# Fourier filter and two-layer MLP on one core: the second transform stage and the stage behind the filter as four 64x64 tiles of TensorE

## The chip, the cores and the metric

The kernel runs on one core of one Trainium2 chip. The metric is the device time in microseconds of one execution. The engines are TensorE (PE, with its weight loads as PEld), VectorE (DVE), ScalarE (ACT), GpSimd (POOL) and SyncE (SP, which here only issues DMAs). Each runs its own instructions in program order and waits for the others by semaphores.

## The reference

For each of 8 batches of 3008 tokens by 256 channels: a real FFT along the tokens, a product with a complex filter, and the inverse FFT. The 24064 tokens then go through a two-layer MLP with a leaky ReLU between.

```python
X = np.fft.rfft(x, axis=1)
F = (filt_r + 1j * filt_i)[None, :, :]
y = np.fft.irfft(X * F, n=x.shape[1], axis=1)
x = y.reshape(B * S, D)             # 24064 x 256
h = x @ w_in                        # 256 x 2048
g = np.maximum(0.01 * h, h)
out = g @ w_out                     # 2048 x 256
```

## The kernel before

**The transform.** 3008 is written as N1 x N2 = 94 x 32, so each FFT is two stages of matmuls, and so is each inverse. Only 48 values of k1 are kept, in two sets of 24. A batch from 1 on goes through these groups; each writes one bank of PSUM, which ACT or DVE empties:

- `s1_group` (L254): the first stage, 16 groups of one matmul over 94 rows (L259), copied by ACT (L262) and stored to DRAM (`dz1`, L264).
- `t1_load` (L268): the result comes back turned, so that a column of TensorE's input holds the 32 values of n2 for four quarters (real and imaginary parts of the two sets of k1): `z1`, four places.
- `s2_group` (L302): the second stage, 12 groups of two matmuls of 128x128 by 256 columns (L308). Half of each 128x128 weight is zero, since the two sets of k1 do not mix. The filter is then applied: DVE multiplies the bank by `fb_sb` (L317) and `fa_sb` (L320), two DMAs swap the two 64-partition halves of the first product (L318, L319), and POOL adds (L323).
- `sa_group` (L326): the stage behind the filter, 12 groups of one matmul of 512 columns (L330), copied by ACT (L332) and stored to DRAM (`dz2`, L334).
- `t2_load` (L275) and `sb_group` (L343): back from DRAM, turned again, and the last stage, 16 groups of four matmuls (L351), copied by ACT into `yt` (L341).

**The MLP.** The tokens are taken in 47 chunks of 512. `moe1` (L514) makes two blocks of 128 hidden channels in a wide PSUM bank pair, with the leaky ReLU on ACT behind every second block (L519). From chunk 3 on the second product is made in seven products of half size (`products`, L589) with sums on DVE (L555, and one add for each product).

**The order.** It is written out by hand. Every step is put at a time of a plan, in units of which a chunk has SL = 8, and the program is emitted in the order of these times: `moe1` steps stand 0.5 units apart, the products evenly between them. `plan` (L694) gives the transform groups of a batch their due times (a start and a step for each kind, in PLANS); the loop at L741 takes them in that order, at least GAP = 0.6 units apart, and not before their loads have landed by plan. `soon` puts the follow-up steps (swaps, adds, stores) some units behind.

**The banks.** `bank` (L156) gives out PSUM. "ph" means two wide banks in turn, shared by `moe1`. "pf" means single banks: the one that the plan marks free first is taken, and its mark is moved on by a hold. After the first chunk two single banks are left for all the transform groups (L499, L500); two more serve the products.

```python
i = min(range(len(single)), key=lambda i: frees[i])
t, frees[i] = single[i], max(frees[i], clock["now"]) + hold
```

Batch 0 has an order of its own (`FIRST`), with other tiles; there some matmuls are 128*64, two column halves side by side (L401 and L442).

Of the kernel before, what the change touches and what calls it, by code (L numbers as in the profile page):

```python
# [11 lines left out]
P = 128  # L12
# [8 lines left out]
NC = 24  # L21
Q = 32
R1 = 96
FP = 3


def _build_np_constants(N):
    n1, n2 = np.arange(N1), np.arange(N2)
    h = N2 // 2

    k2 = np.concatenate([np.arange(h), np.arange(N2 - 1, h - 1, -1)])

    sg = np.where(k2 < h, 1.0, -1.0)[None, :]
    th = 2 * np.pi * np.outer(n2, k2) / N2
    co, si = np.cos(th), np.sin(th)

    fwd1 = np.zeros((P, P))
    fwd2 = np.zeros((P, NC, P))
    inv1 = np.zeros((P, N2, N1))
    inv2 = np.zeros((P, P))  # L40

    for s, (qr, qi) in enumerate(((0, 2), (1, 3))):
        k1 = NC * s + np.arange(NC)

        cr, ci = (slice(64 * i + s, 64 * i + 64, 2) for i in range(2))
        r, i = (slice(Q * q, Q * q + Q) for q in (qr, qi))
        ang = 2 * np.pi * np.outer(n1, k1) / N1
        fwd1[:N1, qr * Q : qr * Q + NC] = np.cos(ang)
        fwd1[:N1, qi * Q : qi * Q + NC] = -np.sin(ang)
        for c in range(NC):  # L50
            t = th + 2 * np.pi * n2[:, None] * k1[c] / N
            fwd2[r, c, cr], fwd2[i, c, cr] = np.cos(t), np.sin(t)
            fwd2[r, c, ci], fwd2[i, c, ci] = -np.sin(t) * sg, np.cos(t) * sg

        w = np.where((k1 == 0) | (k1 == N1 // 2), 1.0, 2.0)[:, None] / N1
# [5 lines left out]
        inv2[cr, i], inv2[ci, i] = si.T, (co * sg).T  # L61
    inv2 /= N2
# [9 lines left out]
    return tuple(np.ascontiguousarray(t).astype(np.float16) for t in (fwd2, inv1, small, fwd2t, inv1t))  # L72


@with_exitstack
def kernel(
# [41 lines left out]
    )  # L118

    f2_np, i1_np, small_np, f2t_np, i1t_np = _build_np_constants(N)  # L120
# [4 lines left out]
    i1t_d = nc.inline_tensor(i1t_np, name="inv1t_const")  # L125

    cpool = ctx.enter_context(tc.tile_pool(name="const", bufs=1))
    f2_sb = cpool.tile([P, NC, P], FP16, name="f2_sb")
# [3 lines left out]
    fb_sb = cpool.tile([P, NC, D], FP16, name="fb_sb")  # L132
    w_in_sb = cpool.tile([P, NDT, DFF], FP16, name="w_in_sb")
    w_out_sb = cpool.tile([P, NCT, D], FP16, name="w_out_sb")
    wt_sb = cpool.tile([P, 4, NCH, P], FP16, name="wt_sb")
    x_sb = cpool.tile([P, N2, D], FP16, name="x_sb")
    big = [cpool.tile([P, Q * D], FP16, name=f"big{i}") for i in range(3)]
# [31 lines left out]
    def at(time, f):  # L169
        clock["n"] += 1  # L170
        heapq.heappush(work, (time, clock["n"], f))
# [96 lines left out]
    def t1_load(b, c):  # L268
        def go():
            need(*[("st1", b, h) for h in range(8)], *[("s2", b, 2 * c - 7)] * (c > 3))  # L270
            nc.sync.dma_start(z1[c % 4], turned(dz1[b % 2], N2, c))
            issued.add(("z1", b, c))
        return go

# [51 lines left out]
    def sa_group(b, g):  # L326
        def go():
            ps = bank("pf", 2, D)
            need(("y", b, g), *[("st2", b, g // 2 - 4)] * (g > 7))
            nc.tensor.matmul(ps, inv2, ys.pop((b, g))[:], start=True, stop=True)  # L330
# [5 lines left out]
        return go  # L336

    def quad_copy(h, dt, ps, copy):

# [164 lines left out]
    def moe1(ci, ct):  # L504
        g, j = divmod(ct, 2)
        if ct == 0:
            gts[ci] = gtp.tile([P, NCT, CH], FP16, tag="gt", name=f"gt_c{ci}")
        if j == 0:
            phs[0] = bank("ph", 2, CH)
        ph, t = phs[0], ci * CH  # L510
        while t < (ci + 1) * CH:
            e = min((ci + 1) * CH, (t // N + 1) * N)
            for dt in range(NDT):
                nc.tensor.matmul(ph[:, j, ds(t - ci * CH, e - t)], w_in_sb[:, dt, ts(ct, P)],  # L514
                                 yt[:, dt, ds(t % N, e - t)],
                                 start=(dt == 0), stop=(dt == NDT - 1))
            t = e
        if j == 1:
            nc.scalar.activation(gts[ci][:, ds(2 * g, 2), :], ph, AF.Lrelu)  # L519
# [174 lines left out]
    def plan(b, s1, s1_step, s2, s2_step, lag, sb, sb_step, xl, x_step):  # L694
        for g in range(16):
            groups.append((s1 + s1_step * g, 1, b, g, s1_group(b, g, dve if b == 1 and g % 4 < 3 else act)))
            if g % 2 and b + 1 < B:
                at(s1 + xl + x_step * g, lambda g=g: (need(("s1", b, g)), noted(
                    ("x", b + 1, g // 2), lambda: x_load(b + 1, 2 * g - 2, 4))))
        for g in range(12):  # L700
            groups.append((s2 + s2_step * g, 2, b, g, s2_group(b, g)))
            groups.append((s2 + lag + s2_step * g, 3, b, g, sa_group(b, g)))
        first_use[1, b], first_use[3, b] = s2, sb
        for g in range(16):
            due = SL * (QT * (8 * b + g // 2) // CH)
            groups.append((min(sb + sb_step * g, due - DUE[0] + DUE[1] * (g % 2)), 4, b, g, sb_group(b, g, act)))

    for i, (o, i0, i1) in enumerate(wt_sums):
        at(10 + 0.5 * i, lambda o=o, i0=i0, i1=i1: nc.vector.tensor_tensor(o, i0, i1, AL.subtract))

# [17 lines left out]
    def load_time(stage, b, c):  # L728
# [7 lines left out]
            at(t, (t1_load if stage == 1 else t2_load)(b, c))  # L736
        return loads[stage, b, c]

    queue = [(time, n, *v) for n, (time, *v) in enumerate(groups)]
    heapq.heapify(queue)  # L740
    while queue:  # L741
        time, n, stage, b, g, f = heapq.heappop(queue)
        t = max(time, last + GAP)
        if stage == 3:
            behind = when[2, b, g] + y_delay(b, g) + 0.02 if (2, b, g) in when else None
        else:
            behind = load_time(stage - 1, b, g // 2) if stage != 1 else 0
            if stage != 1 and behind is not None:
                behind += READ
        if behind is None or behind + 0.02 > t:  # L750
            heapq.heappush(queue, (t + GAP if behind is None else behind + 0.03, n, stage, b, g, f))
# [5 lines left out]
        assert stage < 4 or t < SL * (QT * (8 * b + g // 2) // CH), (b, g, t)  # L757

    for ci in range(NCHUNK + 1):
# [45 lines left out]
```

## Time and profile before

| | |
|---|---|
| time, median of 3 runs | 746.75 us (746.65 to 747.35) |
| the profiled execution's own time | 747.4 us |
| its span, first to last instruction | 745.2 us |
| PE busy | 738.0 us, 99% of the span |
| PE weight loads | 528.9 us, 71% |
| DVE, ACT, POOL busy | 504.6, 559.1, 166.2 us |
| granted clock of TensorE | 0.999 |
| DMA | 113.64 MB, mean 152 GB/s |

Busy times are unions of an engine's instructions. Matmuls are pipelined, so a row's mean duration (379 ns for 512 columns) is longer than the time from one start to the next. In the timeline a row gives the start, the length from the first start to the last end, and how many instructions were merged. In the windows each engine has its busy time and its number of instructions, then follow the clock, the mean share of the DMA engines that is busy (packets can overlap, so over 1 is possible) and GB/s. Lines are those of the kernel before.

### The profile page before, as it was taken

To read this page: it belongs to the slowest core of one execution; us is meant where nothing else is said; L and a number is where in the kernel's file an instruction comes from. 1 tells how busy PE (TensorE), PEld (TensorE's weight loads), DVE (VectorE), ACT (ScalarE), POOL (GpSimd) and SP (SyncE) were. 2 spreads that over 40 slices of the span, in tenths; PEclk is the share of its full clock that TensorE was granted. 3 is DMA by queue.
4 is the path that set the end of the run, shared out by engine and by line. 5 is a ranking of instruction groups with operands and counts; after the bars stand their busy time and mean duration, and the time that the engine had idled before them with its cause. 6 is when DMAs were issued, how large, how long until landed. Compare 5 with 4: busy or idle time off the path is not lost.

```text
span 745.2 us, 19416 instructions
## 1 busy us (share of the span) xinstructions
PE 738.0 (99%) x8017; PEld 528.9 (71%) x8017; DVE 504.6 (68%) x686; ACT 559.1 (75%) x755; POOL 166.2 (22%) x171
## 2 busy tenths in 40 slices
PE   9999999999999999999999999999999999999997
PEld 3556667677687777877778777777777777777776
DVE  5987637766776766766777667766677676465566
ACT  4776787888878787877777787787777777777762
POOL 6503412332232212121232222121212210000000
PEclk9999999999999999999999999999999999999999
DMA  9997797888876666655675656543554333111012
GB/s 207 229 224 197 191 224 216 209 195 208 216 181 147 159 186 176 169 138 163 193 178 150 159 155 175 156 139 109 144 160 119 106 103 103 60 55 55 29 46 70
DMA packets 119848, 113.64 MB, mean 152 GB/s; under 512 B 16384, under 2 KB 93056, under 8 KB 119568
## 3 DMA queue, kind: packets, MB, share of 16 engines
q1 hardware_dynamic: 104425, 94.73, 42.9%
q0 software_dynamic: 15056, 17.49, 15.8%
q8 instruction: 62, 1.02, 0.6%
q14 instruction: 26, 0.21, 0.1%
q10 hardware_dynamic: 279, 0.19, 0.1%
HBM read 57.51 MB, written 50.33 MB: 145 GB/s over the span
## 4 chain that ended last, share of the span: by engine, by line
PE 96%; DMA 1%; DVE 1%; ACT 1%; issue 0%; ACTq 0%; DVEq 0%
PE ph L514 43%; PE pf L589 18%; PE po_ps L589 18%; PE pf L259 3%; PE pf L351 3%; PE pf L308 2%; PE pf L330 2%; PE po_ps L373 1%; PE pf L681 1%; PE po_ps L681 1%; DMA dz<-big 1%; DMA big<-dz 0%; ACT yt L341 0%; PE pf L442 0%; PE ph L401 0%
## 5 line engine op out<-in xcount | busy, mean ns | idle before, releaser
L519 ACT ACTIVATE gt_c<-ph 128x1024 f16<-128x1024 f32 x376 | 385.3, 1025 | 133.5 <-PE ph L514 122.8
L514 PE MATMUL ph<-yt,w_in_sb 128*128 128x512 f16 (+7 forms) x1728 | 447.3, 351 | 0.2 <-ACT yt L341 0.2
L589 PEld LDWEIGHTS <-gt_c 128*128 128x128 f16 x2800 | 202.2, 98 | 91.1
L323 POOL TENSOR_TENSOR y_b_g<-p_b_g,p_b_g 128x512 f16<-128x512 f32 x84 | 116.4, 1388 | 414.9 <-DMA p_b_g<-p_b_g 249.9
L589 PEld LDWEIGHTS <-big 128*128 128x128 f16 x2128 | 151.2, 98 | 61.4
L514 PEld LDWEIGHTS <-w_in_sb 128*128 128x128 f16 x1728 | 137.5, 98 | 19.7 <-DVE yt L341 0.4
L317 DVE TENSOR_TENSOR p_b_g<-pf,fb_sb 128x512 f32<-128x512 f32 x78 | 53.7, 688 | 31.0 <-PE pf L308 13.8
L589 PE MATMUL po_ps<-wt_sb,gt_c 128*128 128x128 f16 x704 | 70.0, 219 | 0.0
L589 PE MATMUL pf<-wt_sb,gt_c 128*128 128x128 f16 x688 | 68.4, 219 | 0.0
L589 PE MATMUL pf<-w_out_sb,gt_c 128*128 128x128 f16 x720 | 67.9, 219 | 0.0
L589 PE MATMUL pf<-wt_sb,big 128*128 128x128 f16 x704 | 67.2, 219 | 0.0
L262 ACT CAST big<-pf 128x512 f16<-128x512 f32 x98 | 57.1, 588 | 11.9 <-PE pf L259 10.5
L589 PE MATMUL po_ps<-w_out_sb,gt_c 128*128 128x128 f16 x688 | 66.0, 219 | 0.0
L589 PE MATMUL po_ps<-wt_sb,big 128*128 128x128 f16 x688 | 65.3, 219 | 0.0
L341 ACT CAST yt<-pf 128x376 f16<-128x376 f32 x120 | 56.4, 473 | 10.9 <-PE pf L351 8.0
L555 DVE TENSOR_TENSOR big<-gt_c 128x2048 f16<-128x2048 f16 (+1 forms) x46 | 58.7, 1276 | 0.1
L555 DVE TENSOR_TENSOR gt_c<-gt_c 128x2048 f16<-128x2048 f16 x43 | 57.4, 1335 | 1.0
L320 DVE TENSOR_TENSOR p_b_g<-pf,fa_sb 128x512 f32<-128x512 f32 x84 | 57.2, 681 | 0.2
L555 DVE TENSOR_TENSOR big<-gt_c,big 128x2048 f16<-128x2048 f16 (+1 forms) x45 | 55.3, 1230 | 0.0
L555 DVE TENSOR_TENSOR big<-big,gt_c 128x2048 f16<-128x2048 f16 (+1 forms) x45 | 55.2, 1227 | 0.1
L332 ACT CAST big<-pf 128x512 f16<-128x512 f32 x84 | 49.0, 584 | 4.9 <-PE pf L330 3.0
L259 PE MATMUL pf<-x_sb,small_sb 94*128 94x512 f16 x109 | 41.6, 381 | 0.0
(97 smaller groups left out, 625.9 us busy)
## 6 DMA issues: line engine op xcount, KB each, us to landing
dz<-big SPq DMA_DIRECT2D x98, 256.0 KB
p_b_g<-p_b_g SPq DMA_DIRECT2D x156, 128.0 KB
out_dram<-ost_c_h SPq DMA_DIRECT2D x118, 128.0 KB
big<-dz SPq DMA_DIRECT2D x42, 256.0 KB
big<-dz SPq DMA_DIRECT2D x56, 192.0 KB
x_sb<-in_x_dram POOLq DMA_DIRECT2D x40, 192.0 KB, 4.4
x_sb<-in_x_dram POOLq DMA_DIRECT2D x2, 768.0 KB, 9.1
w_in_sb<-in_moe_w_in_dram POOLq DMA_DIRECT2D x1, 1024.0 KB, 13.2
```

Source lines behind the costliest of these rows:

```text
L259: nc.tensor.matmul(ps, fwd1[:N1], x_sb[:N1, ds(2 * g, 2), :], start=True, stop=True)
L262: copy(st[:, ds(2 * (g % 2), 2), :], ps)
L317: nc.vector.tensor_tensor(p2[:], ps, fb, AL.mult)
L320: nc.vector.tensor_tensor(p1[:], ps, fa, AL.mult)
L323: ("y", b, g), lambda: nc.gpsimd.tensor_tensor(y1[:], p1[:], p3[:], AL.add)))
L332: nc.scalar.copy(st2[h % 4][:, ds(2 * (g % 2), 2), :], ps)
L341: copy(yv, ps.rearrange("p c a -> p a c"))
L351: nc.tensor.matmul(ps[:, j, :], z2[h % 4][:K4, j, ts(dt, P)], i1_sb[:K4, 4 * h + j, :], start=True, stop=True)
L514: nc.tensor.matmul(ph[:, j, ds(t - ci * CH, e - t)], w_in_sb[:, dt, ts(ct, P)], yt[:, dt, ds(t % N, e - t)], start=(dt == 0), stop=(dt == ...
L519: nc.scalar.activation(gts[ci][:, ds(2 * g, 2), :], ph, AF.Lrelu)
L555: nc.vector.tensor_tensor(*(v[:, ds(c0, n)] for v in (o, i0, i1)), op)
L589: nc.tensor.matmul(of[t], a()[:, c, ts(t, P)], w[:, c, :], start=(c == 0), stop=(c == NCH - 1))
```

## The change

From batch 2 on (`QUARTERS = 2`) `s2_group` and `sa_group` are gone. In their place 37 visits stand at fixed times of the plan (`VISITS`). A visit makes the second stage of four pairs of k1 (`forward`) and, of the visit before, the stage behind the filter (`backward`), with weights of 64x64: TensorE's rows are split by the set of k1, its columns by the parity of the pair, so four tiles stand side by side. The quarters are arranged anew, so that a set's real and imaginary parts are neighbours, and the turned load follows.

- `forward` takes both single banks, with holds of 1.0 and 2.0, and issues 8 matmuls of 256 columns.
- `filtered`, once for each bank, the second 1.05 units later: two multiplies on DVE, four swaps of 32 partitions instead of two of 64, one add on POOL.
- `backward` takes a wide bank pair and issues 4 matmuls of 512 columns; one ACT copy of 128x1024 empties it.
- Other groups keep away from a visit, from 0.9 units before to 1.0 after (`AROUND`); the three `moe1` steps behind a visit are moved on by 0.35, 0.1 and 0.1 (`PAIRS`).
- `refills`, from 29.4 on: the filter tables are loaded again in the new arrangement (eight casting DMAs on POOL's queue, two DMAs between partitions on SP's, four negations on DVE), and two weight tables (SP).

```diff
-    for s, (qr, qi) in enumerate(((0, 2), (1, 3))):
+    for s, (qr, qi) in enumerate(((0, 1), (2, 3))):
...
+    QUARTERS = 2
+    VISITS = (44.75, 49.75, 55.75, 60.75, 65.75, 71.75) + tuple(8 * c + 4.75 for c in range(9, 40))
+    AROUND = (0.9, 1.0)
+    HOLDS = (1.0, 2.0)
+    PAIRS = (0.35, 0.1, 0.1)
+    SECOND = 1.05
+    ADDED = 1.4
+    STORED = 1.2
+    REFILL = 29.4
...
+            if b >= QUARTERS:
+                src = bass.AP(tensor=src.tensor, offset=src.offset, ap=[[Q * D, 4], [P * D, N2], [1, 4 * D]])
...
+    def refill(dst, src, par, k, first, sgn):
+        nc.gpsimd.dma_start(
+            dst[H * par + 16 * k : H * par + 16 * k + 16],
+            bass.AP(tensor=src.tensor, offset=src.offset + (first + sgn * par) * D,
+                    ap=[[N1 * D, N2 // 2], [sgn * NC * D, 2], [sgn * 2 * D, NC // 2], [1, D]]))
+    def refills():
+        t = REFILL
+        for dst, src in ((fb_sb, filt_i), (fa_sb, filt_r)):
+            for par in range(2):
+                for k, (first, sgn) in enumerate(((0, 1), (N1, -1))):
+                    at(t, lambda v=(dst, src, par, k, first, sgn): refill(*v))
+                    t += 0.7
+        for par in range(2):
+            lo = H * par
+            at(t + 2.5, lambda lo=lo: nc.sync.dma_start(fa_sb[lo + Q : lo + H], fa_sb[lo : lo + Q]))
+            for k in range(2):
+                v = ts(k, NC // 2)
+                at(t + 2 + 1.1 * (2 * par + k), lambda lo=lo, v=v: nc.vector.tensor_scalar(
+                    fb_sb[lo + Q : lo + H, v], fb_sb[lo : lo + Q, v], -1.0, None, AL.mult))
+        at(REFILL, lambda: nc.sync.dma_start(i2q_sb[:], i2q_d.ap()))
+        at(REFILL, lambda: noted(("f2q",), lambda: nc.sync.dma_start(f2q, f2q_d.ap())))
+    def forward(b, v):
+        need(("z1", b, v), ("f2q",))
...
+        ps = [bank("pf", 2, D, hold) for hold in HOLDS]
+        for j in range(2):
+            for s in range(2):
+                for par in range(2):
+                    c = 2 * j + par
+                    nc.tensor.matmul(ps[s][ts(par, H), j, :], f2q[ts(s, H), 4 * v + c, :],
+                                     z1[v % 4][ts(s, H), c, :], start=True, stop=True)
+        for s in range(2):
+            if s:
+                soon(SECOND, lambda: filtered(b, v, 1, ps[1]))
+            else:
+                filtered(b, v, 0, ps[0])
+    def filtered(b, v, s, ps):
+        p1, p2, p3 = (scrp.tile([P, 2, D], FP32, tag=f"p{i}", name=f"p{i}_b{b}_v{v}{s}") for i in (1, 2, 3))
+        nc.vector.tensor_tensor(p2[:], ps, fb2[:, s, ds(2 * v, 2), :], AL.mult)
+        for lo in range(0, P, Q):
+            to = lo ^ Q
+            soon(AFTER[1], lambda lo=lo, to=to: nc.sync.dma_start(p3[to : to + Q], p2[lo : lo + Q]))
+        nc.vector.tensor_tensor(p1[:], ps, fa2[:, s, ds(2 * v, 2), :], AL.mult)
+        ys[b, v, s] = y = ypp.tile([P, 2, D], FP16, tag="y", name=f"y_b{b}_v{v}{s}")
+        soon(ADDED, lambda: noted(("yq", b, v, s), lambda: nc.gpsimd.tensor_tensor(y[:], p1[:], p3[:], AL.add)))
+    def backward(b, v):
+        need(("yq", b, v, 0), ("yq", b, v, 1), *[("st2", b, v - 4)] * (v > 3))
+        ps = bank("ph", 2, CH)
+        y = [ys.pop((b, v, s)) for s in range(2)]
+        for par in range(2):
+            for s in range(2):
+                nc.tensor.matmul(ps[ts(s, H), par, :], i2q_sb[ts(par, H), :],
+                                 y[s][ts(par, H)].rearrange("p j d -> p (j d)"), start=True, stop=True)
+        nc.scalar.copy(st2[v % 4].rearrange("p (j w) d -> p w j d", w=2), ps.rearrange("p w (j d) -> p w j d", j=2))
+        soon(STORED, lambda: noted(("st2", b, v), lambda: nc.sync.dma_start(
+            dz2[b % 2][ds(4 * v, 4)].rearrange("k p d -> p k d"), st2[v % 4])))
+    def visit(i):
+        b, v = QUARTERS + i // 6, i % 6
+        if b < B:
+            forward(b, v)
+        if i:
+            backward(b - (v == 0), (v - 1) % 6)
...
-        t = max(time, last + GAP)
+        t = max([time, last + GAP] + [v + AROUND[1] for v in visits if -AROUND[0] < max(time, last + GAP) - v < AROUND[1]])
...
+    later = {}
+    for t in visits[1:]:
+        for n, v in enumerate(PAIRS):
+            later[2 * int(t) + 2 + n] = v
...
-                at(SL * ci + 0.5 * ct, lambda ci=ci, ct=ct: moe1(ci, ct))
+                at(SL * ci + 0.5 * ct + later.get(NCT * ci + ct, 0), lambda ci=ci, ct=ct: moe1(ci, ct))
```

More of the change, by code (lines that the diff above doesn't have):

```diff
@@ L23 @@
 R1 = 96
+H = 64
 FP = 3
@@ L40, in _build_np_constants @@
     inv2 = np.zeros((P, P))
-    for s, (qr, qi) in enumerate(((0, 2), (1, 3))):
+    fwd2q = np.zeros((P, NC, H))
+    inv2q = np.zeros((P, H))
+    for s, (qr, qi) in enumerate(((0, 1), (2, 3))):
         k1 = NC * s + np.arange(NC)
@@ L53, in _build_np_constants @@
             fwd2[r, c, ci], fwd2[i, c, ci] = -np.sin(t) * sg, np.cos(t) * sg
+            fwd2q[r, c, :Q], fwd2q[i, c, :Q] = np.cos(t), np.sin(t)
+            fwd2q[r, c, Q:], fwd2q[i, c, Q:] = -np.sin(t) * sg, np.cos(t) * sg
         w = np.where((k1 == 0) | (k1 == N1 // 2), 1.0, 2.0)[:, None] / N1
@@ L61, in _build_np_constants @@
         inv2[cr, i], inv2[ci, i] = si.T, (co * sg).T
+        inv2q[r, :Q], inv2q[i, :Q] = co.T / N2, -(si * sg).T / N2
+        inv2q[r, Q:], inv2q[i, Q:] = si.T / N2, (co * sg).T / N2
     inv2 /= N2
@@ L71, in _build_np_constants @@
     fwd2 = fwd2.reshape(P, FP, NC // FP, P).transpose(1, 0, 2, 3)
-    return tuple(np.ascontiguousarray(t).astype(np.float16) for t in (fwd2, inv1, small, fwd2t, inv1t))
+    return tuple(np.ascontiguousarray(t).astype(np.float16) for t in (fwd2, inv1, small, fwd2t, inv1t, fwd2q, inv2q))
 @with_exitstack
@@ L118 @@
     )
-    f2_np, i1_np, small_np, f2t_np, i1t_np = _build_np_constants(N)
+    f2_np, i1_np, small_np, f2t_np, i1t_np, f2q_np, i2q_np = _build_np_constants(N)
     f2_d = nc.inline_tensor(f2_np, name="fwd2_const")
@@ L125 @@
     i1t_d = nc.inline_tensor(i1t_np, name="inv1t_const")
+    f2q_d = nc.inline_tensor(f2q_np, name="fwd2q_const")
+    i2q_d = nc.inline_tensor(i2q_np, name="inv2q_const")
     cpool = ctx.enter_context(tc.tile_pool(name="const", bufs=1))
@@ L134 @@
     w_out_sb = cpool.tile([P, NCT, D], FP16, name="w_out_sb")
+    i2q_sb = cpool.tile([P, H], FP16, name="i2q_sb")
     wt_sb = cpool.tile([P, 4, NCH, P], FP16, name="wt_sb")
@@ L270, in go @@
             need(*[("st1", b, h) for h in range(8)], *[("s2", b, 2 * c - 7)] * (c > 3))
-            nc.sync.dma_start(z1[c % 4], turned(dz1[b % 2], N2, c))
+            src = turned(dz1[b % 2], N2, c)
+            if b >= QUARTERS:
+                src = bass.AP(tensor=src.tensor, offset=src.offset, ap=[[Q * D, 4], [P * D, N2], [1, 4 * D]])
+            nc.sync.dma_start(z1[c % 4], src)
             issued.add(("z1", b, c))
@@ L336, in sa_group @@
         return go
+    f2q = f2_sb[:].rearrange("p (a c) m -> p a c m", a=2)[:, 0].rearrange("p c (e m) -> p (c e) m", e=2)
+    fa2, fb2 = (f[:].rearrange("p (s j) d -> p s j d", s=2) for f in (fa_sb, fb_sb))
+    def refill(dst, src, par, k, first, sgn):
[3 more added lines that the diff above has]
+                    ap=[[N1 * D, N2 // 2], [sgn * NC * D, 2], [sgn * 2 * D, NC // 2], [1, D]]))
@@ new lines, in forward @@
+    def forward(b, v):
+        need(("z1", b, v), ("f2q",))
+        for g in (2 * v, 2 * v + 1):
+            issued.add(("s2", b, g))
+        ps = [bank("pf", 2, D, hold) for hold in HOLDS]
[10 more added lines that the diff above has]
+                filtered(b, v, 0, ps[0])
@@ L699, in plan @@
                     ("x", b + 1, g // 2), lambda: x_load(b + 1, 2 * g - 2, 4))))
[L700 to L703, printed above, removed]
+        if b < QUARTERS:
+            for g in range(12):
+                groups.append((s2 + s2_step * g, 2, b, g, s2_group(b, g)))
+                groups.append((s2 + lag + s2_step * g, 3, b, g, sa_group(b, g)))
+        first_use[1, b], first_use[3, b] = s2 if b < QUARTERS else VISITS[6 * (b - QUARTERS)], sb
         for g in range(16):
@@ L706, in plan @@
             groups.append((min(sb + sb_step * g, due - DUE[0] + DUE[1] * (g % 2)), 4, b, g, sb_group(b, g, act)))
+    refills()
     for i, (o, i0, i1) in enumerate(wt_sums):
@@ L737, in load_time @@
         return loads[stage, b, c]
+    visits = VISITS[: 6 * (B - QUARTERS) + 1]
+    for i, t in enumerate(visits):
+        at(t, lambda i=i: visit(i))
+        for g in range(2):
+            when[2, QUARTERS + i // 6, 2 * (i % 6) + g] = t
+    for b in range(QUARTERS, B):
+        when[3, b, 11] = visits[6 * (b - QUARTERS) + 6] + STORED - AFTER[4]
     queue = [(time, n, *v) for n, (time, *v) in enumerate(groups)]
@@ L757 @@
         assert stage < 4 or t < SL * (QT * (8 * b + g // 2) // CH), (b, g, t)
+    for i, t in enumerate(visits):
+        b, v = QUARTERS + i // 6, i % 6
+        if b < B:
+            ready = load_time(1, b, v)
+            assert ready is not None and ready + READ < t, (b, v, ready, t)
+            place[1, v % 4] = t + 0.1
+    later = {}
+    for t in visits[1:]:
+        for n, v in enumerate(PAIRS):
+            later[2 * int(t) + 2 + n] = v
     for ci in range(NCHUNK + 1):
```

## The prediction

> **What bounds the kernel now.** I read the page first, then the groups by form of the tensor engine (PE), its timeline around the only column-tiled matmuls, the timelines of PE and the scalar engine (ACT) in one steady stretch, the chain of waits around 100 us, and the windows there.
>
> ```profile
> span 745.2 us, 19416 instructions
> PE 738.0 (99%) x8017; PEld 528.9 (71%) x8017; DVE 504.6 (68%) x686; ACT 559.1 (75%) x755; POOL 166.2 (22%) x171
> ...
> PE 96%; DMA 1%; DVE 1%; ACT 1%; issue 0%; ACTq 0%; DVEq 0%
> ```
>
> PE is both the busy engine and 96% of the chain that ended last. From 150 us to 700 us the windows show it busy for 50.00 us in every 50, at a granted clock of 1.00. So a PE microsecond saved is one off the span, and a PE wait added is one on it; no other engine hides either.
>
> ```profile
> L308 PE MATMUL pf<-big,f_sb 128*128 128x256 f16 x168 | 32.1, 273 | 0.2 <-ACT big L262 0.2
> L330 PE MATMUL pf<-y_b_g,small_sb 128*128 128x512 f16 x84 | 31.8, 379 | 0.0
> ```
>
> L308 is the second transform stage, L330 the one behind the filter. Mean durations overlap their neighbours; what one costs is its busy time added to a full engine. In the timeline below two L514 matmuls start at 270.94 and the next work at 271.37, so 512 columns cost 0.216 us. Seven L589 matmuls take 269.51 to 269.90: 0.056 us for 128 columns. 256 columns are then 0.109.
>
> **Part 1, the tiles: what PE gains.** Two old groups are four L308 and two L330 matmuls: 4 x 0.109 + 2 x 0.216 = 0.868 us. One visit is eight matmuls of 256 columns, in two rounds of four tiles, and four of 512 in one round: 2 x 0.109 + 0.216 = 0.434 us if four 64x64 tiles stream together. The trace has no 64-row matmul. The nearest rows are column tiles (128*64):
>
> ```profile
> 21.43 0.60 PE L425 MATMUL pf<-prod,small_sb 128*128 128x512 f16 x2
> 21.96 0.65 PE L401 MATMUL ph<-big,f_sb 128*64 128x128 f16 x16
> 22.55 0.60 PE L425 MATMUL pf<-prod,small_sb 128*128 128x512 f16 x2
> 23.09 0.64 PE L401 MATMUL ph<-big,f_sb 128*64 128x128 f16 x16
> 23.66 0.61 PE L425 MATMUL pf<-prod,small_sb 128*128 128x512 f16 x2
> ```
>
> From 22.55 to 23.66 is 1.11 us, for 2 x 0.216 and eight column pairs. If a pair costs the 0.056 of one matmul, that is 0.88, and 0.23 is left for leaving and re-entering the full array. Were pairs serial, 16 x 0.056 alone would exceed the 0.57 between 23.09 and 23.66. So column halves do run together, and each visit pays 0.23 for its two switches (forward and backward share one stay). Bounds for a round of four: 0.109 if row halves overlap as column halves do, 0.218 if they do not. I take the first, because the two row halves read different partitions and write different banks. Saving: 0.868 - 0.434 - 0.23 = 0.20 us, times 36, less 0.23 for the 37th visit: **-7.1 us**.
>
> The Trainium skill (TensorE: Matmul & The Clock Gate, Part 3) gives 3.07 times for four row tiles, not 4. By that, as an estimate, a visit would stream 0.57 and the saving would be some 2 us. No run here shows it.
>
> **Part 2, the banks: what PE waits for.** This is where I expect the loss. Only two single banks are left for all transform groups after the list is cut at SL - 0.4. A visit takes both, with holds of 1.0 and 2.0 plan units (a unit is 1/8 chunk, about 1.9 us: chunks start 15.2 us apart around 300 us). AROUND keeps every other group out from 0.9 before to 1.0 after. I laid the due times of s1_group and sb_group (the plan's starts and steps) against VISITS by the diff's own rule. 36 of 37 visits get a group A at exactly +1.0, and 27 a second, B, at +1.6. Example: visit 132.75; sb of batch 3, g=1, is due at 132.68 and goes to 133.75; s1 of batch 5, g=8, is due at 133.75 and goes 0.6 behind it, to 134.35. A takes the first bank (free by plan at +1.0) and marks it to +1.75. B chooses the smaller mark, 1.75 against 2.0, so the bank A has just filled, 0.6 units later. Before, two neighbours alternated, and no bank came back under 1.2 units.
>
> On PE, between the starts of A and B lie A itself (0.18 for four L351, 0.22 for one L259), eight products (0.45) and one moe1 step (0.43): **1.06 or 1.10 us**. How long A holds the bank is seen here, first PE, then ACT:
>
> ```profile
> 270.94 0.59 PE L514 MATMUL ph<-yt,w_in_sb 128*128 128x512 f16 x2
> 271.37 0.39 PE L589 MATMUL po_ps<-w_out_sb,gt_c 128*128 128x128 f16 x4
> 271.59 0.38 PE L259 MATMUL pf<-x_sb,small_sb 94*128 94x512 f16 x1
> ```
> ```profile
> 271.57 1.02 ACT L519 ACTIVATE gt_c<-ph 128x1024 f16<-128x1024 f32 x1
> 272.49 0.58 ACT L262 CAST big<-pf 128x512 f16<-128x512 f32 x1
> ```
>
> The second half of a moe1 pair ends just before the group, so its 1.02 us activation stands ahead of the group's copy on ACT, and the bank is free at 273.07, 1.48 us after the matmul started. In a visit PAIRS puts that half at +0.85 and A at +1.0, so two products lie between instead of four, and the copy ends 0.11 later: 1.59 for s1. For sb the copy is 473 ns instead of 588 (L341 and L262 on the page): 1.48. With 0.05 for the semaphore (a copy of the chain ends at 64.92, its matmul starts at 64.97), B waits 0.54 us behind an s1 and 0.47 behind an sb. By the plan A is s1 8 times and sb 19 times: 8 x 0.54 + 19 x 0.47 = **+13.3 us**. Bounds: nothing, if A and B fall further apart than I count; 27 x 0.65 = 18 if ACT is later still.
>
> The Trainium skill (TensorEngine Tiling, PSUM Bottleneck) warns that tiling speeds up TensorE and not the emptying of PSUM. The rows above agree: the copies keep their length while PE comes sooner.
>
> Other waits of a visit I set at nothing, with their cover. The wide bank for the backward half was read one pair earlier; the bank of the pair before is due back 1.53 us after that pair's last matmul starts (0.216 + 4 products + the visit + 8 products) and takes 0.416 + 1.02 to empty: tight, and 0.1 x 37 = 4 us if it slips. DVE keeps two multiplies per half. ACT gives up two copies of 584 ns for one of 1025.
>
> **Part 3, the refills.** At 29.4 (91 us) eight cast DMAs enter POOL's queue, 192 KB each, and four transfers SP's. They fall on a stretch with no slack:
>
> ```profile
> 100.69 5.51 DMA dz<-big
> 106.21 2.98 DMA big<-dz
> ```
> ```profile
> 95.00:100.00 5.00, 5.00 (x41) 3.14 (x40) 3.11 (x4) 4.61 (x8) 1.98 (x4) 1.00 1.00 190
> 100.00:105.00 5.00, 5.00 (x48) 3.21 (x47) 2.44 (x3) 5.00 (x9) 0.00 (x0) 1.00 1.08 275
> 105.00:110.00 5.00, 4.84 (x53) 3.20 (x52) 1.26 (x3) 4.23 (x7) 0.00 (x0) 1.00 0.64 184
> ```
>
> DMA share is 1.0 already, and PE waits 0.16 us for the last of batch 1's z2 loads at 109.2. 1.6 MB of refills at the 190 to 275 GB/s seen is 6 to 8 us of transfer within some 14 us. On POOL's queue the refills also stand ahead of the last y add of batch 1 (94.2, read at 99.3) and of an x load issued at 95.5. Bounds 0 and +8, since other transfers may absorb all of it; I take **+2**, nearer nothing, because the load falls to 0.64 right behind.
>
> **Part 4, the swaps and loads.** SP issues eight swaps of 32 partitions per visit instead of four of 64. Its timeline gives about 0.5 us for each, so +2 us of issue per visit on a queue whose issues fill some 27 of 50 us (31 between 150 and 200). Behind them queue z loads and output stores. Batch 2's visits stand 5 or 6 units apart, some 10 us, and the second y is ready about 9 us after its visit (filter +2, multiply 1.4, four issues 2, landing 2, add 1.4). From batch 3 on the gap is 15 us. The last backward of a batch moves to the next batch's first visit, so z2 loads come just in time at five batch ends. Bounds 0 and +5; I take **+1.5**.
>
> **Sum.** The profiled execution took 747.4 (span 745.2 and 2.2 around it), 0.65 above the median 746.75. 747.4 - 7.1 + 13.3 + 2 + 1.5 = 757.1; less 0.65, **756.5 us**.
>
> **Rivals.** *The gain comes through*: B falls later than I count or ACT is earlier, and the refills hide. For it: PE's saving is plain arithmetic, and DVE, ACT and SP all have spare time on average. Against: the bank rule and the ACT order. Time: 746.75 - 7.1 = 739.7, up to 745 with the small waits. It decides if fewer than 7.1 / 0.5 = 14 visits have a waiting B. *Row halves do not overlap*: streaming stays 0.868 and the switches are added, 37 x 0.23 = +8.5; alone 755, with the banks and the rest 772. For it: no row shows 64-row tiles; against it, column halves do overlap. *A draw*: about half of the bank waits, within 0.2% of 746.75; that much is about what a measurement of this kernel can tell from no change.
>
> **Chances.** Bank waits outweigh the saving 0.60; row halves serial 0.09 (slower too); gain 0.26; draw 0.05. The range 740 to 767 takes in the gain almost whole, the draw, and the forecast with its bounds on banks and refills, and leaves out most of the serial case. For the likeliest case alone it is 749 to 767.
>
> **What would show it.** Right: matmuls of L259 and L351 behind visits with idle time ended by ACT, some 27 gaps of 0.45 to 0.65 us, PE's busy share below 50.00 from 150 us on, and visits about 0.66 us long. Refill wrong: the sb matmul near 109 us not later. Saving wrong: rounds of four taking 0.22. The forecast falls if PE stays gapless between 150 and 640 us.

## The result, and the profile after

The changed kernel took **835.39 us** (median of 6 runs, 831.93 to 837.25) against 747.35 for the kernel before: ratio 1.1178 [1.1153, 1.1202]. It is 88 us slower; the forecast was 756.5 in a range of 740 to 767. The profiled execution has a span of 832.8 us, 87.6 more than before.

First the page of the kernel after: the span, the busy times, and the chain that ended last.

```profile
span 832.8 us, 20090 instructions
PE 757.5 (91%) x8233; PEld 530.3 (64%) x8233; DVE 521.0 (63%) x690; ACT 555.0 (67%) x719; POOL 174.3 (21%) x179
...
PE 74%; DMA 17%; issue 3%; ACT 2%; SPq 2%; POOL 1%; DVE 1%; POOLq 0%; ACTq 0%; DVEq 0%
```

PE was 96% of the chain and is 74%; DMA went from 1% to 17%, the DMA queue of SP from nothing to 2%. Next the groups by form: behind the second bar the idle time of PE ahead of them, and what ended it.

```profile
L278 PE MATMUL pf<-x_sb,small_sb 94*128 94x512 f16 x109 | 42.6, 391 | 8.5 <-DMA x_sb<-in_x_dram 5.3 <-ACT yt L435 3.2
L445 PE MATMUL pf<-i_sb,big 96*128 96x94 f16 x448 | 39.4, 211 | 26.7 <-DMA big<-dz 22.3 <-ACT big L281 2.6 <-ACT yt L435 1.8
L419 PE MATMUL ph<-y_b_v,i2q_sb 64*64 64x512 f16 x144 | 16.8, 390 | 21.0 <-POOL y_b_v L411 21.0
L395 PE MATMUL pf<-big,f_sb 64*64 64x256 f16 x288 | 15.1, 284 | 11.5 <-DMA big<-dz 11.5
```

L395 is `forward`, L419 `backward`, L445 `sb_group`, L278 `s1_group`. "big<-dz" is a load of `z1` or `z2`; L411 is POOL's add, which needs the swapped halves. So some 55 us of PE's idle time (22.3 + 21.0 + 11.5) hang on turned loads and swaps, and only 3.2 + 2.6 + 1.8 = 7.6 on ACT, where the forecast put the loss. The windows show where PE's clock went too (the columns are those of the windows before; the clock stands third from last):

```profile
200.00:250.00 50.00, 36.26 (x380) 24.48 (x378) 24.10 (x34) 26.41 (x34) 9.04 (x9) 0.83 0.56 146
250.00:300.00 50.00, 49.02 (x582) 35.60 (x579) 34.73 (x45) 38.34 (x51) 13.06 (x14) 1.00 0.63 155
300.00:350.00 50.00, 43.32 (x454) 29.66 (x452) 27.86 (x38) 31.65 (x42) 8.45 (x7) 0.90 0.50 139
...
540.00:545.00 5.00, 0.66 (x8) 0.66 (x9) 0.00 (x0) 0.12 (x1) 2.52 (x2) 0.54 0.59 173
```

The loss comes in lumps, at the ends of batches; the stretch in between, 250 to 300, is nearly full. All eight waits of 3.6 us or more, and three of the five between 1.8 and 3.2, come with a granted clock of 0.5, most of them for 3.4 or 6.8 us (the last line falls in such a stretch), so a long wait is paid twice. The Trainium skill (TensorE: Matmul & The Clock Gate, Part 1) states half rate after an idle window of about 3.4 us. The lengths here agree with such a window, the waits only in part: one of 1.85 us (at 324.0) had the half clock behind it, one of 3.13 us (at 132.6) had not.

For the account I took the time from each matmul's start to the next one's, less the median for the same form in the kernel before, and put the excess down to what ended the wait (that of a whole visit to its longest wait). The terms add up to the 87.6 us:

| term | us | forecast |
|---|---|---|
| waits for y in a visit (4, for swaps that are issued or land late) | +26.2 | in "the swaps and loads", 1.5 in all |
| waits for z2 ahead of `sb_group` (5) | +23.1 | the same 1.5 |
| waits for z1 in a visit | +9.6 | the same 1.5 |
| PE at half clock behind waits | +19.1 | not thought of |
| bank waits, released by ACT (24) | +11.6 | 13.3 |
| a wait for x at 104 to 110 us, in the reload | +5.5 | 2 |
| the tiles, 37 visits (23.76 for 31.2) | -7.5 | -7.1 |

One batch end shows the mechanism. From the chain of waits of the kernel after (start, length, what):

```profile
522.40 0.51 SPq L293
522.96 13.18 DMA big<-dz
...
536.16 0.51 SPq L408
536.76 4.68 DMA dz<-big
541.51 2.79 DMA big<-dz
544.35 0.50 PE pf L445 x4
```

L293 issues a z1 load, L408 a swap. The fourth z1 load of the next batch takes 13.18 us. The visit itself is hardly late (it starts at 526.53, after 0.29 us of waiting), but on SP's queue its swaps come ahead of the store of its result (`dz<-big`). A swap is issued at 536.16, as soon as that z1 load has landed at 536.14, the store behind it, z2 can be loaded only then, and the PE timeline (start, length, work, and in brackets idle time and its releaser) ends in a hole:

```profile
537.83 0.28 PE L683 MATMUL pf<-w_out_sb,gt_c 128*128 128x128 f16 x2
544.35 0.50 PE L445 MATMUL pf<-i_sb,big 96*128 96x94 f16 x4 [6.24 <-DMA big<-dz]
544.63 0.74 PE L683 MATMUL pf<-w_out_sb,gt_c 128*128 128x128 f16 x5
```

While that load ran, the DMA engines were not full (0.19 to 0.59 in windows of 2 and 3 us from 523 to 536); two of these windows, with the share as the last number but one:

```profile
523.00:525.00 2.00, 2.00 (x21) 1.32 (x20) 1.34 (x3) 1.75 (x3) 0.00 (x0) 1.00 0.19 66
...
531.00:533.00 2.00, 2.00 (x25) 1.50 (x24) 0.42 (x1) 1.38 (x3) 0.00 (x0) 1.00 0.26 94
```

Why does a swap wait for a load that it has nothing to do with? In the trace, SP's DMAs raise eight semaphores in turn, and nearly every issue (724 of 752) waits until the DMA before it on its own semaphore, nearly always the eighth before it on the queue, has landed. So a late load holds up the whole queue at the eighth issue behind it. From SP's waits of the kernel after (who waits for what: us in all, times, longest):

```profile
SPq L408 <- DMA big<-dz: 20.9, 15, 2.0
```

All of SP's waits for such loads come to 29.8 us here, and to 0.7 in the kernel before.

And why is a load slow in a DMA system that is not full? In the semaphore events of the trace, a z1 load raises its semaphore 16 times before the change (last update 3.9 us after the issue, median). After it, from batch 2 on, it does so 5 times: once 1.0 us after the issue, and four times later, the last at 9.8 us (median; about 6 alone, 13 for the fourth of four). Its size is 256 KB in both. What changed is the order of its pattern: it begins with the four quarters, where before it began with the 32 values of n2.

The Trainium skill (DMA: Bandwidth & Descriptors, Why a DMA increments its semaphore by 16 and not by 1) states that a DMA is split over as many engines, up to 16, as divide the slowest dimension of both its patterns, and that the engines not used are credited to the semaphore at once. A slowest dimension of 4 then means four engines; the 1 + 4 updates agree with it. The swaps behind also land late once they are issued: 41 of 288 took more than 5 us, the longest 11.1. That they do so because they need those same four engines is argued from this rule, not read from the trace, which doesn't tell the engine of a packet.

### The profile page after: what moved, and what is told of

The parts are those of the page before. It is cut to its first block, busy times and chain, and to the rows that moved or that the text cites. A ratio compares the mean times of both kernels' runs of the same rounds, so it can differ in the third digit from the quotient of the medians.

```text
span 832.8 us, 20090 instructions
## 1 busy us (share of the span) xinstructions
PE 757.5 (91%) x8233; PEld 530.3 (64%) x8233; DVE 521.0 (63%) x690; ACT 555.0 (67%) x719; POOL 174.3 (21%) x179
## 3 DMA queue, kind: packets, MB, share of 16 engines
q8 instruction: 64, 1.05, 0.5%
## 4 chain that ended last, share of the span: by engine, by line
PE 74%; DMA 17%; issue 3%; ACT 2%; SPq 2%; POOL 1%; DVE 1%; POOLq 0%; ACTq 0%; DVEq 0%
PE ph L608 34%; PE pf L683 14%; PE po_ps L683 14%; DMA big<-dz 10%; DMA dz<-big 4%; PE pf L445 2%; PE pf L278 2%; DMA p_b_v<-p_b_v 2%; PE pf L775 1%; PE pf L395 1%; PE po_ps L775 1%; ACT yt L435 1%; DMA x_sb<-in_x_dram 1%; SPq L408 1%; PE ph L419 1%
## 5 line engine op out<-in xcount | busy, mean ns | idle before, releaser
L608 PE MATMUL ph<-yt,w_in_sb 128*128 128x512 f16 (+7 forms) x1728 | 457.7, 358 | 0.2 <-ACT yt L435 0.2
L683 PEld LDWEIGHTS <-gt_c 128*128 128x128 f16 x2800 | 204.8, 100 | 102.0 <-issue 13.6
L411 POOL TENSOR_TENSOR y_b_v<-p_b_v,p_b_v 128x512 f16<-128x512 f32 x72 | 104.4, 1450 | 464.2 <-DMA p_b_v<-p_b_v 321.0
L683 PEld LDWEIGHTS <-big 128*128 128x128 f16 x2128 | 148.2, 99 | 69.3 <-issue 14.8
L281 ACT CAST big<-pf 128x512 f16<-128x512 f32 x98 | 57.0, 586 | 20.1 <-PE pf L278 19.7
L445 PE MATMUL pf<-i_sb,big 96*128 96x94 f16 x448 | 39.4, 211 | 26.7 <-DMA big<-dz 22.3
L649 DVE TENSOR_TENSOR gt_c<-gt_c 128x2048 f16<-128x2048 f16 x43 | 62.5, 1452 | 1.4
L405 DVE TENSOR_TENSOR p_b_v<-pf,fb_sb 128x512 f32<-128x512 f32 x72 | 49.4, 686 | 19.9 <-PE pf L395 10.3
L649 DVE TENSOR_TENSOR big<-big,gt_c 128x2048 f16<-128x2048 f16 (+1 forms) x45 | 58.3, 1295 | 0.1
L421 ACT CAST big<-ph 128x1024 f16<-128x1024 f32 x36 | 36.3, 1008 | 31.0 <-PE ph L419 31.0
L278 PE MATMUL pf<-x_sb,small_sb 94*128 94x512 f16 x109 | 42.6, 391 | 8.5 <-DMA x_sb<-in_x_dram 5.3
```

Of the source, the lines that this page charges most:

```text
L278: nc.tensor.matmul(ps, fwd1[:N1], x_sb[:N1, ds(2 * g, 2), :], start=True, stop=True)
L281: copy(st[:, ds(2 * (g % 2), 2), :], ps)
L405: nc.vector.tensor_tensor(p2[:], ps, fb2[:, s, ds(2 * v, 2), :], AL.mult)
L411: soon(ADDED, lambda: noted(("yq", b, v, s), lambda: nc.gpsimd.tensor_tensor(y[:], p1[:], p3[:], AL.add)))
L421: nc.scalar.copy(st2[v % 4].rearrange("p (j w) d -> p w j d", w=2), ps.rearrange("p w (j d) -> p w j d", j=2))
L445: nc.tensor.matmul(ps[:, j, :], z2[h % 4][:K4, j, ts(dt, P)], i1_sb[:K4, 4 * h + j, :], start=True, stop=True)
```

## The experiments

**Theory**: the z1 load's order of dimensions is the main cause, the swaps on SP's queue the second. **Rivals**: the reload of the filter tables; the bank waits of the forecast; the eight swaps alone. Diffs are against the kernel after unless told otherwise. Times are medians, ratios to the kernel before (747.3 to 748.4 us beside them) with 95% intervals.

### The load's order: put right in the kernel after, and put wrong in the kernel before

*Spread load*: z1 comes as two DMAs of 64 partitions whose patterns begin with the 32 values of n2; the rows of `f2q` are reordered to fit. Bytes and everything else are as in the kernel after, but for one more issue for each load.

```diff
+    fwd2q = fwd2q.reshape(2, 2, Q, NC, H).transpose(0, 2, 1, 3, 4).reshape(P, NC, H)
...
-                src = bass.AP(tensor=src.tensor, offset=src.offset, ap=[[Q * D, 4], [P * D, N2], [1, 4 * D]])
-            nc.sync.dma_start(z1[c % 4], src)
+                for i in range(2):
+                    nc.sync.dma_start(z1[c % 4][ts(i, H)], bass.AP(
+                        tensor=src.tensor, offset=src.offset + 2 * i * Q * D,
+                        ap=[[P * D, N2], [Q * D, 2], [1, 4 * D]]))
+            else:
+                nc.sync.dma_start(z1[c % 4], src)
```

> The changed kernel, its turned load made as two DMAs of 64 partitions whose source pattern begins with 32 rows instead of 4 (the rows of the 64x64 weights are put in the same order). Theory A (the turned load of the changed kernel runs on 4 DMA engines and its lateness starts nearly all of the loss): the waits at L395 and the long ones of the backward half and of the last stage go, the granted clock returns to 0.99 or more, and the time is 747.4 less 7.3 for the tiles, plus 7.7 for the bank waits, plus 7.8 for the waits near 110 us, so 753 to 762 us. Theory B (the extra swaps on SP's queue and the refills are the cause): the long waits stay and the time is above 800 us.

*Slow load alone*: the kernel before, with nothing but that order in batches 1 to 7, and its weight table in the same order.

```diff
-    fwd2t = fwd2.reshape(4, Q, NC, P).transpose(1, 0, 2, 3).reshape(P, NC, P)
+    fwd2t = fwd2.reshape(P, NC, P)
...
-            nc.sync.dma_start(z1[c % 4], turned(dz1[b % 2], N2, c))
+            src = turned(dz1[b % 2], N2, c)
+            nc.sync.dma_start(z1[c % 4], bass.AP(
+                tensor=src.tensor, offset=src.offset, ap=[[Q * D, 4], [P * D, N2], [1, 4 * D]]))
```

> The kernel before, with nothing changed but the order of the turned load of the second stage (source pattern beginning with 4 quarters, for batches 1 to 7) and the rows of its weights to match. Theory A: each load lands 6 us after its issue and four in a row 13 us, PE waits at most batch starts, 765 to 800 us. Theory B: no more than 1 us from the kernel before.

Measured: spread load **797.56**, 1.0668 [1.0635, 1.0702]; slow load alone **799.55**, 1.0683 [1.0659, 1.0706]. The order of one load's dimensions costs 51 us without any tile (0.0683 of 748, in seven batches where the change has it in six), and taking it out of the change gives back 38 (0.1178 - 0.0668). That is the largest single part, but not nearly all: 797.56 lies far above the 753 to 762 expected, waits for y and z2 are left, and the granted clock is 0.985. With the spread load the semaphore gets 16 updates from each half again, and the last comes 2.8 us after the issue. In the kernel before with the slow load, the largest loss isn't at the stage that reads z1. The groups by form:

```profile
L332 PE MATMUL pf<-y_b_g,small_sb 128*128 128x512 f16 x84 | 32.9, 391 | 31.5 <-POOL y_b_g L325 31.4
L310 PE MATMUL pf<-big,f_sb 128*128 128x256 f16 x168 | 32.6, 276 | 3.8 <-DMA big<-dz 3.5 <-ACT big L262 0.2
```

and one step of its chain of waits:

```profile
380.92 2.43 SPq L320
383.40 10.61 DMA p_b_g<-p_b_g
394.17 1.27 POOL y_b_g L325
```

A swap lands after 10.61 us there; in the kernel before the medians of the two swaps are 2.8 and 2.9 and the longest 6.8. The slow load is hidden for itself (3.5 us of waits) and delays the small transfers that follow it (31.4).

### The reload and the banks

Without the reload of the filter tables, on top of the spread load:

```diff
-                    at(t, lambda v=(dst, src, par, k, first, sgn): refill(*v))
...
-            at(t + 2.5, lambda lo=lo: nc.sync.dma_start(fa_sb[lo + Q : lo + H], fa_sb[lo : lo + Q]))
...
-                at(t + 2 + 1.1 * (2 * par + k), lambda lo=lo, v=v: nc.vector.tensor_scalar(
-                    fb_sb[lo + Q : lo + H, v], fb_sb[lo : lo + Q, v], -1.0, None, AL.mult))
```

> The first kernel of this call, without the reload of the filter tables (eight casting DMAs, two copies, four negations); the filter values of batches 2 to 7 are then those of the old arrangement. Theory A with the refill priced at 7.8 us: the waits near 105 to 120 us go, 7 to 8 us under the first kernel. If the DMAs of the refill are hidden once the loads are quick: within 1 us of it.

With the spread load, and the second group behind a visit kept 1.2 units from the first, so that the bank just filled has time to empty:

```diff
-        when[stage, b, g] = last = t
+        when[stage, b, g] = t
+        last = t + GAP * any(abs(t - v - AROUND[1]) < 0.01 for v in visits if v > 76)
```

> The first kernel of this call, with the group after the first one behind a visit (from batch 3 on) put 1.2 units behind it instead of 0.6, so that no bank is taken again after 0.6 units. The waits of L278 and L445 on ACT's copies measured 0.32 us each in the changed kernel, some 18 of them from there on: 5 to 6 us under the first kernel. If the group's delay brings other waits: no gain.

Measured: no reload **788.13**, 1.0525 [1.0490, 1.0560]; bank gap **791.74**, 1.0589 [1.0545, 1.0633]. The reload costs 9.4 us. Windows of the spread load with the reload, then without it:

```profile
105.00:110.00 5.00, 1.64 (x18) 1.06 (x16) 1.37 (x2) 1.77 (x3) 0.59 (x2) 1.00 1.26 223
```
```profile
105.00:110.00 5.00, 4.17 (x41) 2.64 (x39) 1.12 (x2) 4.06 (x6) 0.00 (x0) 1.00 0.70 187
```

PE stands for 3.4 of 5 us at a DMA share of 1.26, and for 0.8 at 0.70. The bank gap takes the bank waits from 13.1 us (27 of them) to 2.4, and moves other groups: 2.4 us of new waits of `moe1` on ACT, and the net gain is 5.8 us. Both are clear of the noise, and both are small beside 88.

### The swaps

Spread load, and the swaps issued on POOL's queue instead of SP's, with the add 0.55 units later:

```diff
-    ADDED = 1.4
+    ADDED = 1.95
...
-            soon(AFTER[1], lambda lo=lo, to=to: nc.sync.dma_start(p3[to : to + Q], p2[lo : lo + Q]))
+            soon(AFTER[1], lambda lo=lo, to=to: nc.gpsimd.dma_start(p3[to : to + Q], p2[lo : lo + Q]))
```

> The changed kernel with the spread turned load, and the eight swaps of a visit issued from POOL's queue instead of SP's (the adds put behind the swaps of both halves: ADDED 1.95). Theory C (after the load, SP's queue is the cause: a DMA of 32 partitions costs it 0.59 us as one of 64 does, so a visit's swaps hold it for 4.7 us, and the stores, the loads of the last stage and the swaps themselves come late): the waits of L450 on big<-dz (13.1 us) and most of the waits of the backward half on y in batch 2 shrink, and with them the half clock; 765 to 785 us, against 797.6 with the swaps on SP. Theory D (the waits come from the planned distances alone, the y and the last load being due too early whoever issues): 790 to 805 us.

The same two edits on the kernel after, with the slow load kept:

> The changed kernel with its own slow load, only the swaps moved from SP's queue to POOL's (ADDED 1.95). Theory A+C (the slow load's packets hold four engines of SP's hardware queue, and what SP issues behind them waits its turn, swaps first of all): the waits of the backward half on y (26 us) mostly go, those on the z1 loads stay: 780 to 805 us, more than half of the gain of both repairs together (835 to 770). If swaps wait for the engines themselves, whatever their queue: 815 to 835 us.

And the kernel before, with its swaps cut in four DMAs of 32 partitions instead of two of 64:

```diff
-                soon(AFTER[1], lambda: nc.sync.dma_start(p3[0:64], p2[64:P]))
-                soon(AFTER[1], lambda: nc.sync.dma_start(p3[64:P], p2[0:64]))
+                for lo in range(0, P, Q):
+                    to = lo ^ 64
+                    soon(AFTER[1], lambda lo=lo, to=to: nc.sync.dma_start(p3[to : to + Q], p2[lo : lo + Q]))
```

> The kernel before with each swap of 64 partitions made as two of 32, for all its batches: 156 more issues on SP's queue, the same bytes, nothing else. Theory C: SP's issue time rises by some 0.55 us x 156 = 86 us, from 27 to some 35 of 50 us; the plan's distances to the last stage are longer here than in the changed kernel, so PE waits less: 750 to 765 us. Theory D: 747 to 749 us.

Measured: spread load with swaps on POOL **769.60**, 1.0279 [1.0258, 1.0300]; the kernel after with swaps on POOL **817.60**, 1.0914 [1.0886, 1.0942]; split swaps before **751.79**, 1.0047 [1.0032, 1.0062]. So the number of swaps costs 3.5 us in the kernel before (0.0047 of 748), and their place on SP's queue 29 us in the changed kernel (0.0668 - 0.0279) or 20 with the slow load still there (0.1178 - 0.0914). No run moves the add alone, so its later place is in these two figures. With the slow load and the swaps on POOL the waits for y fall from 26.2 to 2.8 us, while the visits' waits for z1 stay (12.2 against 9.6) and those for z2 grow (27.7 against 23.1): the swaps are no longer issued behind the slow loads, the rest still is.

The 817.60 us is a miss all the same. It lies outside the 780 to 805 expected and in the range set for swaps that wait for the engines whatever their queue, and the trace bears part of that out. POOL's swaps that are issued while a slow z1 load is under way land after 5.5 us (median of 90), the others after 2.8 (198); with the spread load it is 3.4 (71) against 2.7 (217). So the slow load delays transfers of another queue too. The order on SP's queue and this slowing work together, and no run tells their shares.

SP's timeline at the end of a batch shows what else queues. Spread load, swaps on SP:

```profile
405.04 2.37 SPq L674 DMA_DIRECT2D out_dram<-ost_c_h  x3
407.50 1.20 SPq L294 DMA_DIRECT2D big<-dz  x2
408.80 2.50 SPq L413 DMA_DIRECT2D p_b_v<-p_b_v  x4
411.40 0.53 SPq L427 DMA_DIRECT2D dz<-big  x1
412.04 0.47 SPq L284 DMA_DIRECT2D dz<-big  x1
412.61 3.26 SPq L413 DMA_DIRECT2D p_b_v<-p_b_v  x4
415.97 1.95 SPq L305 DMA_DIRECT2D big<-dz  x4
```

Spread load, swaps on POOL:

```profile
390.40 1.20 SPq L294 DMA_DIRECT2D big<-dz  x2
391.69 0.54 SPq L427 DMA_DIRECT2D dz<-big  x1
392.33 0.53 SPq L284 DMA_DIRECT2D dz<-big  x1
396.00 1.74 SPq L305 DMA_DIRECT2D big<-dz  x4
```

L427 stores the last result of a batch, L305 loads z2 from it. With the swaps on SP, four of them stand between the z1 loads and the store, and four more between the store and the z2 loads. The backward half of the visit began at 403.7, the z2 loads are issued 12.3 us later, and PE waits 4.0 us for them at 418.75. With the swaps on POOL the backward half began at 387.8, the store follows the z1 loads at once, the z2 loads are issued after 8.2 us, and PE doesn't wait for them.

### Putting the repairs together: five misses

*Spread load, swaps on POOL, bank gap, no reload* (the edits above).

> All the repairs at once: spread load, swaps on POOL's queue, 1.2 units behind the first group after a visit from batch 3 on, and no reload of the filter tables (so the filter values of batches 2 to 7 are those of the old arrangement). If these four are the whole loss, what is left is the tiles' gain of 7.3 us and some 2 us of bank waits in batch 2: 740 to 745 us. If the distances of the visits themselves cost (Theory D), above 760 us.

*Spread load, store of the backward half sooner*: `STORED` 1.2 to 0.75 units, to bring z2 forward.

> The spread load, and the store behind the backward half put at 0.75 units instead of 1.2, so that it stands ahead of the visit's swaps on SP's queue. Theory C: the five waits of the last stage on its loads (13.1 us, 2 to 4 us each) shorten by some 2 us each, 785 to 792 us. Theory D: the same, by 0.45 units or 0.85 us each, 792 to 796 us.

*All repairs, with the whole computation*: spread load, swaps on POOL, bank gap, `STORED = 0.75`, `REFILL` 29.4 to 33.0, and the first eight `sb_group`s of a batch 1.3 units later behind their loads.

```diff
-    REFILL = 29.4
+    REFILL = 33.0
...
-                behind += READ
+                behind += READ + 1.3 * (stage == 4 and b >= QUARTERS and g < 8)
```

> The changed kernel with the spread load, the swaps on POOL's queue, 1.2 units behind the first group after a visit from batch 3 on, the reload of the filter tables begun at 33.0 instead of 29.4 (behind the x load that waited for it), the store behind the backward half at 0.75, and 1.3 units more between the last stage's loads and their use for the first eight groups of a batch. All the computation is done. If the loss is made of the waits named so far: 745.2 of span, less 7.5 for the tiles, plus 3 for the reload, 5 for batch 2's y, 5 for banks: 750 to 755 us. If the visits cost something else: above 760 us.

*The same, but visits from batch 3 on*: `QUARTERS = 3`, the visits of batch 3 at 84.75 to 118.75, later ones as before, `REFILL = 75.5`, bank gap behind every visit. (Its first visit multiplies by a part of `fb` whose sign has not been turned yet.)

> The same repairs with the tiles from batch 3 (counted from 0) on, QUARTERS = 3: 31 visits instead of 37, six of them 6 to 7 units apart, the first at 84.75, and the reload at 75.5, away from the stretch near 100 us; the wider step behind a visit's first group holds for all visits. The tiles save 30 x 0.214 less 0.23, or 6.2 us. If the reload and the close visits of batch 2 were what kept the repaired kernel above the one before: 743 to 748 us, at or under it. If the waits move along with the tiles: 750 to 758 us.

*All repairs without the reload*, whose cost they then show by difference:

> The kernel with all repairs and the tiles from batch 2 on, without the reload of the filter tables (the filter values of batches 2 to 7 are those of the old arrangement). With the reload it took 772.5 us and its waits before 145 us (11.8 and 6.4 us, and the half clock behind them) are put down to the reload's DMAs. If that is so, what is left is the tiles' gain of 7.5 us, some 5 us of bank waits and 2 of batch 2's y: 744 to 750 us, the gain used up by the plan around it. If the waits come back elsewhere: above 755 us.

| kernel | us | ratio |
|---|---|---|
| spread, POOL, bank gap, no reload | 761.08 | 1.0161 [1.0133, 1.0188] |
| spread, store sooner | 803.92 | 1.0755 [1.0707, 1.0803] |
| all repairs | 772.51 | 1.0333 [1.0318, 1.0349] |
| all repairs, from batch 3 | 766.05 | 1.0245 [1.0227, 1.0262] |
| all repairs, no reload | 755.73 | 1.0108 [1.0088, 1.0128] |

The first four came out 8 to 18 us above what was expected of them, the last 6 us. The sooner store gained nothing, it lost 6 us, and waits for z2 are 15.3 us where they were 13.1. SP's timeline at a batch end of that kernel:

```profile
310.49 0.54 SPq L427 DMA_DIRECT2D dz<-big  x1
311.14 5.02 SPq L413 DMA_DIRECT2D p_b_v<-p_b_v  x8
316.61 0.38 SPq L284 DMA_DIRECT2D dz<-big  x1
317.04 1.91 SPq L305 DMA_DIRECT2D big<-dz  x4
```

The store (L427) did move ahead of the swaps, but all eight swaps now stand between it and the z2 loads (L305). These are issued 10.8 us behind the backward half (306.2), where with the spread load alone it was 10.7 (305.8 to 316.52): it is the place of the swaps on the queue that counts, and moving the store doesn't change it.

Moving the reload moved its collision. The chain of waits of all repairs, where the reload stands at 33.0:

```profile
102.97 12.28 DMA dz<-big
...
115.26 4.75 DMA big<-dz
120.02 0.05 issue
120.06 0.50 PE pf L450 x4
```

A store of batch 1 takes 12.28 us to land in the reload (DMA share 1.21 from 100 to 120 us), and PE waits 10.91 us behind it, and 6.21 us at 142 us for a bank that DVE's multiply empties late. With the reload at 75.5 two waits went along with it: 5.1 us for z1 at 204 us, and 9.5 at 219 us for a bank that DVE's multiply empties late. That DVE stood there for the tables on POOL's queue, which the swaps now share, is argued and not separated. Without the reload the repaired kernel is 16.8 us faster (0.0333 - 0.0108): it is hidden neither at 29.4 nor at 33.0, and at 75.5 the two waits speak against it, though no run leaves it out there.

In the steady part the repairs do what was expected of them. The window from 300 to 350 us, spread load alone and then all repairs without the reload:

```profile
300.00:350.00 50.00, 46.45 (x540) 34.58 (x539) 32.07 (x43) 35.69 (x46) 10.83 (x11) 0.97 0.66 170
```
```profile
300.00:350.00 50.00, 50.00 (x608) 37.41 (x605) 36.54 (x49) 39.58 (x53) 27.88 (x43) 1.00 0.70 177
```

PE is full again there. Over the whole span this kernel still waits 5.4 us for y (3 waits), 3.2 for `yt` on ACT, 2.2 for z2, 2.4 for banks, and some 1.5 at half clock, together 14.7, which is more than the 7.5 that the tiles bring; the rest, 7.2, is nearly the 7.9 us by which its span is longer than before. Whether a better order would also remove these wasn't tried; no version here beats the kernel before.

## Why the prediction was wrong

**Part 1, the tiles: right.** -7.1 was forecast, -7.5 came. An undisturbed visit takes 0.654 us of PE (0.664 forecast); 27 of the 37 are within 0.015 us of that, or of 0.44 where one half is missing: the two rounds of L395 start 0.11 us apart, so row halves overlap as column halves do, and the rival with serial row halves is out. The 3.07 times for four row tiles (the Trainium skill, TensorE: Matmul & The Clock Gate, Part 3), by which a visit would have been an estimated 0.80 with the switches, doesn't carry over to these 64x64 tiles; the trace decides. The visit in the PE timeline:

```profile
526.53 0.41 PE L395 MATMUL pf<-big,f_sb 64*64 64x256 f16 x8 [0.29 <-DMA big<-dz]
526.75 0.41 PE L419 MATMUL ph<-y_b_v,i2q_sb 64*64 64x512 f16 x4
527.09 0.62 PE L683 MATMUL po_ps<-wt_sb,big 128*128 128x128 f16 x8
...
528.75 0.34 PE L445 MATMUL pf<-i_sb,big 96*128 96x94 f16 x4
530.27 0.38 PE L278 MATMUL pf<-x_sb,small_sb 94*128 94x512 f16 x1 [0.31 <-ACT yt L435]
```

**Part 2, the banks: right in kind and nearly in size.** The last line above is such a wait: the second group behind a visit, ended by ACT, after an L445. In the spread-load kernel there are exactly 27, worth 13.1 us (13.3 forecast; 0.484 each, 0.47 and 0.54 forecast). The gap that the profile shows is 0.31 or 0.38, 0.16 less than the cost, because it counts from the end of the matmul ahead, and a matmul in a full stream lasts that much longer (379 ns for 512 columns) than the time to the next start (216 ns); hence gaps of 0.45 to 0.65 were the wrong thing to look for, though the cost was right. They come behind 8 groups of `s1_group` and 19 of `sb_group`, as the forecast had counted. In the kernel after 24 are left (11.6 us), the others lie in holes that a DMA ended.

**Part 3, the reload: too low.** 2 was taken, with 8 as the upper bound. It costs 9.4 with the spread load and 16.8 with all repairs. The step that failed is the choice of "nearer nothing, because the load falls to 0.64 right behind": the share was already 1.0 where the reload was put, and the loads of batch 1 couldn't wait for the quieter stretch.

**Part 4, the swaps and loads: the step that failed, 59 us against 1.5.** Waits for y, z2 and z1 together are 26.2 + 23.1 + 9.6. Two things were wrong. First, the new pattern of the z1 load was costed at nothing: the text counts the DMAs and their issue, and takes their landing for unchanged. The diff shows the order of dimensions, `[[Q * D, 4], ...]`, and the rule quoted above points at it, though it gives no time; no load of this size in the kernel before has such an order. Alone it is 51 us. Second, the swap issue was costed by the queue's mean (27 of 50 us, and 2 us more a visit), where the batch end needs swaps, store, z2 loads and output stores in turn on the one queue, and each issue there waits for the landing of the eighth before it; that is 20 to 29 us, with the later add in it. "z2 loads come just in time at five batch ends" was written down, and the sum didn't ask what it costs if that cover goes. The bounds, 0 and +5, held no transfer that lands late.

**What was missing altogether**: PE at half clock, 19.1 us, which no part has. It stands behind the long waits, of which the failed term and the wait for x make 64 us, so it adds some 30% to them.

**The rivals.** All three stayed on the scale of the banks and the tiles. None named a queue. What was to show the forecast wrong, a gapless PE between 150 and 640 us, didn't come; the signs named for "right" (idle ended by ACT) did come, and they were an eighth of the loss.

## What to carry to other kernels

When a diff changes an access pattern, cost its landing time and not only its bytes and its issue: read the slowest dimension of source and destination, and compare with a DMA in the trace that has the same one. Count a queue at its fullest place, here the end of a batch where store and load depend on one another through the same queue, and not by its mean, and see how many transfers it keeps in flight: here one late load stopped the eighth issue behind it. A saving of PE time in a kernel that is 99% PE is worth only what its new loads and copies can still keep hidden, and here every wait of 3.6 us or more, and some shorter ones, were paid again in half clock.

## What the hardware showed that I had not expected

- A load of 256 KB whose pattern began with a dimension of 4 landed in about 6 us alone and 13 as the fourth in a row, and raised its semaphore 5 times; beginning with 32, as two halves, 2.8 us and 16 times each. The busy share of the DMA engines was 0.19 to 0.59 while it ran.
- That load delayed transfers issued on another queue: swaps on POOL's queue landed after 5.5 us while one was under way, and after 2.8 otherwise (medians).
- The price of an issue on SP goes by DMA and not by size: 0.585 us for a swap of 32 partitions, 0.52 to 0.59 for one of 64 (medians).
- Behind every wait of 3.6 us or more the granted clock was 0.5 for 3.4 or 6.8 us; at 216 us, where waits followed one another, for 17.1 us. A wait of 1.85 us had it too, one of 3.13 us had not.
- Four 64x64 tiles on different rows, columns and banks start within 10 to 36 ns of each other, and a visit of 12 such matmuls with both switches took 0.654 us.
